# A grouped-query decode step on one core: the last head's output weights on 8 partitions, x for the end in eight loads from GpSimd

## Chip, cores and metric

One core of a Trainium2 chip, everything in float32. The metric is the device time of one execution in microseconds; the kernel before takes 1311.54 us (median of 3 runs, 1311.51 to 1311.91).

## What is computed

```python
def reference(A_x, A_k_cache, A_v_cache, A_wq, A_wo, B_x, B_w1, B_b1, B_w2, B_b2):
    # _A_ref: B=2 rows, Hq=32 heads, Hkv=8, Sk=32768 cached positions, Dh=128, D=512
    q = (x @ wq).reshape(B, Sq, Hq, Dh).transpose(0, 2, 1, 3)
    scores = einsum("bhqd,bhkd->bhqk", q, k) * (Dh ** -0.5)
    p = softmax(scores, axis=-1)
    o = einsum("bhqk,bhkd->bhqd", p, v)
    s = o.transpose(0, 2, 1, 3).reshape(B, Sq, Hq * Dh) @ wo
    # _B_ref: F=1792
    h = x @ w1 + b1
    h = max(h, 0) ** 2
    g = silu(h @ w2 + b2)
    # together; _A_ref is given layernorm(x), _B_ref too
    return x + s * g
```

The caches are 256 MiB each, wq and wo 8 MiB each, w1 and w2 3.5 MiB each; all of them are read once.

## The kernel before

There are 16 sequences `s` (8 key heads times 2 batch rows), each with 32768 cached rows. Keys come as halves of 16384 rows (`load_k`, 8 MB), cut into four tiles `n` for `scores`; values come as two chunks a sequence (`load_v`, 8 MB). All these loads, and those of the weights, are issued by SyncE in the order of the list `loads`; an entry is issued once its event is past (`give`), and `issue` goes on down the list until it meets one whose event is not. One load is split over the 16 DMA engines, 8 partitions each, and each engine works through its share of the queue in order.

Memory: `kslots` is [128, 3, 8192] floats, three slots of 4 MB for keys; `vbuf` is 8 MB for values and, at the start, for wq, w1 and w2. At the end the slots take wo: groups 0 and 1 in slot 2, groups 2 and 3 in slot 0, slot 1 is then free. The last but one value load goes into slots 0 and 1.

`scores(n)` transposes the keys 32x32 on VectorE (L248) and multiplies on TensorE (L253). `softmax` and `probs` make the weights `pT`, `values(n)` multiplies them with the values (L316) and, at the end of a sequence, forms the head outputs `oT` (L327, L328). For every second key head it spreads the 8 heads of a group for the final projection: a product with a selection mask (L332), one matmul (L335) and a copy (L336) bring row 8p+j of the group to partition p, step j of `oW`. This fits a load of wo where partition p holds the 8 consecutive rows 8p to 8p+7.

The final projection `project` (L395 to L403) runs over 4 groups of 8 steps j. A step is four matmuls, one for each quarter `g` of the 512 output columns, which go to four column groups of 32 of the array and so to four partition groups of one accumulator `a_ps`. A float32 matmul appears as two records in the trace, so a step has 8. The last group's weights come in four loads (`PIECES`), of 4, 2, 1 and 1 rows a partition, and are multiplied piece by piece. Then VectorE multiplies with the gate (L406), adds x, which lies in `xe` in the same four partition groups (L407), and two stores go out.

x for the end is loaded in four loads by ScalarE's queue at the start (L78), after b1, b2 and the x of the layer norm. GpSimd clears `oW` at the start (L180) and later, in `set_q`, places the queries of each sequence (L231). VectorE makes the selection masks (L166 to L177) among the steps of the layer norm; the reciprocal of the norm is at L197.

The order of instructions within an engine's queue is made by a scheduler that follows the program's order but moves an instruction into a wait that it foresees. Waits are semaphores; each DMA is given one of eight for SyncE and ScalarE, in turn, and one of eight others when GpSimd issues it.

Of the kernel before, what the change touches and what calls it, by code (L numbers as in the profile page):

```python
# [9 lines left out]
F32 = mybir.dt.float32  # L10
AF = mybir.ActivationFunctionType
ALU = mybir.AluOpType
AX = mybir.AxisListType

P = 128
# [10 lines left out]
NG = 4  # L26
# [3 lines left out]
TS = (1, 0, 2, 3)  # L30
NT = 4
HALF = 64 * 128
PIECES = ((0, 4), (4, 6), (6, 7), (7, 8))


@with_exitstack
def gqa_decode_kernel(ctx: ExitStack, tc: tile.TileContext, x, kc, vc, wq, wo, w1, b1, w2, b2, out):
    nc = tc.nc
    B, _, D = x.shape
    _, HKV, SK, DH = kc.shape  # L40
    HQ = wq.shape[1] // DH
# [7 lines left out]
    DE = D // NG  # L49
    WG = 8  # L50
    NWG = HQ // WG
# [3 lines left out]
    x2 = x.rearrange("b s d -> (b s) d")  # L55
    out2 = out.rearrange("b s d -> (b s) d")

    const = ctx.enter_context(tc.tile_pool(name="const", bufs=1))
    ktpool = ctx.enter_context(tc.tile_pool(name="ktpool", bufs=8))
    work = ctx.enter_context(tc.tile_pool(name="work", bufs=2))  # L60
# [3 lines left out]
    def misc(name):  # L64
        return pms.tile([P, 512], F32, tag="ms", name=name)
# [8 lines left out]
    nc.scalar.dma_start(b2t, b2[None, :])  # L74
    xe = const.tile([P, DE], F32, name="xe")
    nc.gpsimd.memset(xe, 0.0)
    for g in range(NG):
        nc.scalar.dma_start(xe[32 * g:32 * g + B, :], x2[:, g * DE:(g + 1) * DE])  # L78

    tiles = {}  # L80

# [35 lines left out]
        return t.rearrange("p (j e) -> p j e", j=FJ)  # L117


    def load_wo(i):  # L120
        if i % 2 == 0:
            wide[i // 2] = kslots[:, 2 - i].rearrange("p (i j e) -> p i j e", i=2, j=WG)
        t = wide[i // 2][:, i % 2]
        src = wo[i * WG * P:(i + 1) * WG * P, :].rearrange("(p j) e -> p j e", p=P)
        if i < NWG - 1:
            nc.sync.dma_start(t, src)
        else:
            for j0, j1 in PIECES:
                nc.sync.dma_start(t[:, j0:j1, :], src[:, j0:j1, :])  # L129
        return t  # L130

    wide = {}
    NK, NV = NS * NT, NS * NCH
    kslots = const.tile([P, 3, HALF], F32, name="kslots")
    vbuf = const.tile([P, 2 * HALF], F32, name="vbuf")
    loads = [(None, load_wq, 0), (None, load_half, 0), (None, load_half, 1), (("q", 0), load_w1, 0),
             (("s", 0), load_half, 2), (None, load_half, 3), (("q", 0), load_w2, 0)]
    for m in range(2, NV):
        loads += [(("s", 2 * m - 2), load_k, m), (("v", m - 3) if m > 2 else ("w", 1), load_v, m - 2)]
    loads += [(("s", NK - 2), load_v, NV - 2), (("v", NV - 3), load_v, NV - 1)]  # L140
    loads += [(("s", NK - 1), load_wo, 0), (("s", NK - 1), load_wo, 1), (("v", NV - 2), load_wo, 2), (("v", NV - 2), load_wo, 3)]
    past = {None}
    done = [0]
# [7 lines left out]
    def take(f, a):  # L151
        return tiles.pop((f, a))

    def give(*event):
        past.add(event)
        issue()
# [4 lines left out]
    ident = const.tile([P, P], F32, name="ident")  # L161
# [12 lines left out]
    selj = const.tile([P, WG], F32, name="selj")  # L174
    nc.vector.tensor_reduce(selj, ident.rearrange("p (e j) -> p j e", j=WG), axis=AX.X, op=ALU.add)
    sele = const.tile([P, P // WG], F32, name="sele")
    nc.vector.tensor_reduce(sele, ident.rearrange("p (e j) -> p e j", j=WG), axis=AX.X, op=ALU.add)  # L177
    oT = const.tile([P, HQ, B], F32, name="oT")
    oW = const.tile([P, NWG, WG, 32], F32, name="oW")
    nc.gpsimd.memset(oW, 0.0)  # L180
    sc = [pone.tile([P, 512], F32, tag=f"sc{i}", name=f"sc{i}") for i in range(NT)]
    o_ps = [pone.tile([P, 512], F32, tag=f"o{i}", name=f"o_ps{i}") for i in range(2)]
    for t in o_ps:
        nc.vector.memset(t, 0.0)


    st = const.tile([P, 4], F32, name="st")
# [12 lines left out]
    t_ps = misc("xnT_ps")  # L200
# [6 lines left out]
    for d in range(ND):  # L207
        for f in range(2):
            for g in range(NG):
                cc = f * NG + g  # L210
                nc.tensor.matmul(sc[f][32 * g:32 * g + 32, :], xnT[:, d, 0:32], wqt[:, d, cc * 512:(cc + 1) * 512],  # L211
                                 start=(d == 0), stop=(d == ND - 1))
    give("q", 0)
    qT = const.tile([P, B, HKV, REP, 4], F32, name="qT")
    for f in range(2):
        for h in range(REP):
# [3 lines left out]
            t_ps = misc(f"qT_ps{f}_{h}")  # L220
# [87 lines left out]
    def values(n):  # L308
        s, k = divmod(n, NCH)
        vt = take(load_v, n)  # L310
        o = o_ps[s % 2]
        for c in range(2):
            for i in range(NO // 4):
                for g in range(NG):
                    lo = (c * NG + g) * NO + 4 * i
                    nc.tensor.matmul(o[32 * g:32 * g + 16, :], pT[s][:, k, g, c, 4 * i:4 * i + 4, :].rearrange("p o h -> p (o h)"),  # L316
                                     vt[:, lo:lo + 4, :].rearrange("p o d -> p (o d)"),
                                     start=(k + c + i == 0), stop=(k == NCH - 1 and c == 1 and i == NO // 4 - 1))
        give("v", n)
        if k == NCH - 1:  # L320
            hkv, b = divmod(s, B)
            o_sb = work.tile([P, 512], F32, tag="o_sb", bufs=1, name=f"o_sb{s}")
            nc.scalar.copy(o_sb, o)  # L323
            t_ps = misc(f"oT_ps{s}")
            r4 = rs.pop(s)
            for i in range(4):
                nc.tensor.matmul(t_ps[:, :REP], o_sb[:, i * DH:(i + 1) * DH], r4[:, i, :], start=(i == 0), stop=(i == 3))  # L327
            nc.vector.tensor_copy(oT[:, hkv * REP:(hkv + 1) * REP, b], t_ps[:, :REP])  # L328
            if hkv % 2 == 1:
                i = hkv // 2  # L330
                m = work.tile([P, WG, P // WG], F32, tag="om", bufs=1, name=f"om{s}")
                nc.vector.tensor_mul(m, oT[:, i * WG:(i + 1) * WG, b:b + 1].to_broadcast([P, WG, P // WG]),  # L332
                                     sele[:, None, :].to_broadcast([P, WG, P // WG]))
                t_ps = misc(f"oW_ps{s}")
                nc.tensor.matmul(t_ps[:, :WG], m.rearrange("p h e -> p (h e)"), selj, start=True, stop=True)  # L335
                nc.scalar.copy(oW[:, i, :, b], t_ps[:, :WG])  # L336


    hT, gate = first[:, 3, :FJ * 32].rearrange("p (j b) -> p j b", j=FJ), const.tile([P, DE], F32, name="gate")
# [33 lines left out]
    for n in range(NK):  # L373
        s, i = divmod(n, NT)
        if i == 0:
            set_q(s)
        scores(n)
        if n == 1:
            mlp_up()
        if n == 3:  # L380
            mlp_down()
        if i == 3:
            softmax(s)
        if n >= 5 and n % 2 == 1:
            values((n - 5) // 2)
        if i == 3:
            probs(s)
    values(NV - 2)
    values(NV - 1)


    a_ps = sc[0]
    wot = [take(load_wo, i) for i in range(NWG)]

    def project(i, j0, j1):  # L395
        for j in range(j0, j1):
            for g in range(NG):
                nc.tensor.matmul(a_ps[32 * g:32 * g + 32, :DE], oW[:, i, j, :], wot[i][:, j, g * DE:(g + 1) * DE],
                                 start=(i == 0 and j == 0), stop=(i == NWG - 1 and j == WG - 1))

    for i in range(NWG - 1):
        project(i, 0, WG)
    for j0, j1 in PIECES:  # L403
        project(NWG - 1, j0, j1)
    asb = work.tile([P, DE], F32, tag="e", bufs=1, name="a_sb")
    nc.vector.tensor_mul(asb, gate, a_ps[:, :DE])  # L406
    nc.vector.tensor_add(xe, asb, xe)  # L407
# [25 lines left out]
```

## Time and profile before

| | |
|---|---|
| median of 3 runs | 1311.54 us |
| the profiled execution | 1311.62 us |
| its span | 1309.61 us |
| mean granted clock of TensorE | 0.841 of full speed |
| TensorE busy (matmul) | 885.4 us, 68% |
| VectorE busy | 648.8 us, 50% |
| ScalarE busy | 88.3 us, 7% |
| GpSimd busy | 15.1 us, 1% |
| read from memory | 561.01 MB, 428 GB/s over the span |
| SyncE's queue (q1) | 99.2% of the time of 16 DMA engines |

The span is what the profile covers; the execution is some 2 us longer. Busy shares are means over the whole span: an engine at 68% can still be the one that ends last in a stage, and in this profile the waits of the last 75 us are what tells. The chain of waits is the sequence of work that ended last, followed back from the end. The clock is what TensorE was granted; the last 10 us ran at 1.00.

### The profile page before, as it was taken

How to read it: one execution, taken by the hardware profiler on the slowest of the kernel's cores; microseconds unless marked ns; L12 is line 12 of the kernel's file. 1: busy time of each engine (PE TensorE's matmuls, PEld its weight loads, DVE VectorE, ACT ScalarE, POOL GpSimd, SP SyncE). 2: the span in 40 equal slices, each digit the busy share in tenths (PEclk: the TensorE clock that was granted, in tenths of full speed). 3: DMA queues.
4: the chain of work that ended last, by engine and by line, in shares of the span. 5: the costliest groups of instructions: out<-in, count | busy, mean ns of one | idle time of the engine just before them, and what ended most of it. 6: DMA issues, size and time to landing. Idle time of an engine off the chain costs nothing.

```text
span 1309.6 us, 11506 instructions
## 1 busy us (share of the span) xinstructions
PE 885.4 (68%) x4926; PEld 251.1 (19%) x4926; DVE 648.8 (50%) x742; ACT 88.3 (7%) x237; POOL 15.1 (1%) x76
## 2 busy tenths in 40 slices
PE   3867675658757567775657766566875756776575
PEld 1222121112212111121212211111221211112123
DVE  2855654435555344655435565443655534465410
ACT  0010010101001010000101001010000101000010
POOL 0000000000000000000000000000000000000000
PEclk9988877888878788877789978778987878888788
DMA  9999999999999999999999999999999999999997
GB/s 403 433 441 439 424 439 423 441 433 431 435 427 435 435 427 443 423 439 428 437 429 431 435 427 443 419 443 429 435 435 427 439 427 437 435 425 441 421 441 303
DMA packets 11040, 561.74 MB, mean 429 GB/s; under 512 B 1239, under 2 KB 1259, under 8 KB 1646
## 3 DMA queue, kind: packets, MB, share of 16 engines
q1 hardware_dynamic: 10952, 561.00, 99.2%
q8 instruction: 38, 0.62, 0.2%
q14 instruction: 12, 0.10, 0.0%
q10 hardware_dynamic: 38, 0.02, 0.0%
HBM read 561.01 MB, written 0.00 MB: 428 GB/s over the span
## 4 chain that ended last, share of the span: by engine, by line
DMA 74%; DVE 18%; issue 5%; PE 2%; SPq 0%; DVEq 0%
DMA kslots<-in_A_k_cache 68%; DVE kt L248 18%; DMA kslots<-in_A_wo 2%; DMA kslots<-in_A_v_cache 2%; DMA vbuf<-in_A_wq 2%; PE sc L211 1%; PE o_ps L316 0%; PE h_ps L347 0%; SPq L129 0%; DVE qr L218 0%; DVEq L248 0%; PE qT_ps L222 0%; PE sc L253 0%; DVE h L354 0%; DVE first L355 0%
## 5 line engine op out<-in xcount | busy, mean ns | idle before, releaser
L253 PE MATMUL sc<-kt,qz 128*32 128x512 f32 x2048 | 578.4, 671 | 330.6 <-DVE kt L248 309.0
L248 DVE STREAM_TRANSPOSE kt<-kslots 128x1024 f32<-128x1024 f32 x512 | 580.7, 1205 | 350.9 <-DMA kslots<-in_A_k_cache 350.9
L253 PEld LDWEIGHTS sc<-kt,qz 128*32 128x32 f32 x2048 | 112.0, 115 | 783.1 <-DVE kt L248 580.7
L316 PE MATMUL o_ps<-vbuf,pT 128*16 128x512 f32 x1984 | 228.8, 597 | 11.0 <-DMA vbuf<-in_A_v_cache 11.0
L316 PEld LDWEIGHTS o_ps<-vbuf,pT 128*16 128x16 f32 x1984 | 76.7, 97 | 139.9 <-issue 119.6
L275 ACT ACTIVATE p<-sc,nm 128x512 f32<-128x512 f32 x32 | 23.3, 746 | 991.0 <-DVE nm L271 991.0
L328 DVE COPY oT<-oT_ps 128x4 f32<-128x4 f32 x16 | 2.6, 162 | 121.5 <-PE oT_ps L327 121.5
L258 DVE TENSOR_REDUCE rm<-sc 128x1 f32<-128x512 f32 x32 | 22.1, 691 | 63.9 <-PE sc L253 63.9
L294 ACT COPY pT<-pT_ps 64x256 f32<-64x256 f32 x128 | 46.8, 366 | 19.7 <-PE pT_ps L290 18.2
L300 DVE RECIPROCAL r<-l_ps 128x4 f32<-128x4 f32 x16 | 2.9, 182 | 46.2 <-PE l_ps L298 46.2
L231 POOL COPY qz<-qT 32x16 f32<-32x16 f32 x64 | 12.7, 198 | 1077.4 <-PE sc L253 1042.5
L327 PE MATMUL oT_ps<-rs,o_sb 128*128 128x4 f32 x128 | 16.9, 255 | 11.5 <-ACT o_sb L323 11.4
L290 PE MATMUL pT_ps<-ident,p 128*128 128x128 f32 x128 | 20.2, 309 | 2.9 <-ACT p L275 2.9
L327 PEld LDWEIGHTS oT_ps<-rs,o_sb 128*128 128x128 f32 x128 | 15.5, 191 | 25.6 <-ACT o_sb L323 25.6
L298 PE MATMUL l_ps<-lh,ones 128*128 128x4 f32 x32 | 8.2, 327 | 17.6 <-ACT pT L294 17.6
L290 PEld LDWEIGHTS pT_ps<-ident,p 128*128 128x128 f32 x128 | 17.4, 169 | 3.1 <-ACT p L275 3.1
L323 ACT COPY o_sb<-o_ps 128x512 f32<-128x512 f32 x16 | 9.4, 585 | 100.1 <-PE o_ps L316 100.1
L278 DVE TENSOR_REDUCE l<-l 128x1 f32<-128x2 f32 x16 | 2.5, 155 | 26.9 <-ACT p L275 26.9
L264 PE MATMUL mx_ps<-ident,rm 128*128 128x128 f32 x16 | 5.2, 323 | 14.6 <-DVE rm L262 14.6
L202 PE MATMUL xnT_ps<-ident,xn 128*128 128x128 f32 x4 | 1.1, 428 | 20.4 <-DVE xn L198 20.4
L316 PE MATMUL o_ps<-kslots,pT 128*16 128x512 f32 x64 | 8.4, 682 | 4.2 <-DMA kslots<-in_A_v_cache 4.2
L298 PEld LDWEIGHTS l_ps<-lh,ones 128*128 128x128 f32 x32 | 6.8, 266 | 22.0 <-ACT pT L294 22.0
(68 smaller groups left out, 116.2 us busy)
## 6 DMA issues: line engine op xcount, KB each, us to landing
kslots<-in_A_k_cache SPq DMA_DIRECT2D x4, 4096.0 KB, 20.8
vbuf<-in_B_w SPq DMA_DIRECT2D x2, 3584.0 KB
kslots<-in_A_wo SPq DMA_DIRECT2D x3, 2048.0 KB
kslots<-in_A_wo SPq DMA_DIRECT2D x1, 1024.0 KB
kslots<-in_A_wo SPq DMA_DIRECT2D x1, 512.0 KB
kslots<-in_A_wo SPq DMA_DIRECT2D x2, 256.0 KB, 31.3
vbuf<-in_A_v_cache SPq DMA_DIRECT2D x31, 31.0
kslots<-in_A_k_cache SPq DMA_DIRECT2D x30
```

The costliest lines, as they stand in the source:

```text
L211: nc.tensor.matmul(sc[f][32 * g:32 * g + 32, :], xnT[:, d, 0:32], wqt[:, d, cc * 512:(cc + 1) * 512], start=(d == 0), stop=(d == ND - 1))
L231: nc.gpsimd.tensor_copy(qz[s % 2][32 * a:32 * a + 32, 16:].rearrange("p (e y) -> p e y", e=4)[:, :, a * REP:(a + 1) * REP], qT[32 * a:32 * ...
L248: nc.vector.transpose(r.rearrange("p e o w -> p o e w"), kt[:, g * NO:(g + 1) * NO, e0 * 32:(e0 + 2) * 32].rearrange("p o (e w) -> p o e w ...
L253: nc.tensor.matmul(bank[32 * g:32 * g + 32, :], qz[s % 2][:, lo + 32 * (e0 + e):lo + 32 * (e0 + e) + 32], kts[g][:, e].rearrange("p o w -> ...
L258: nc.vector.tensor_reduce(rm[s][:, u:u + 1], bank, axis=AX.X, op=ALU.max)
L275: nc.scalar.activation(p[:, :, :, u], sc[2 * (s % 2) + u].rearrange("p (o w) -> p o w", w=32), AF.Exp, bias=nm, scale=SCALE, accum_out=l2[ ...
L290: nc.tensor.transpose(t_ps[:, j * P:(j + 1) * P], p[:, o:o + 2].rearrange("p o w u -> p (o w u)"), ident)
L294: nc.scalar.copy(sb[64 * a:64 * a + 64].rearrange("p k g c (i j o) h -> p i o j (g c) k h", i=2, o=2)[:, i, o], v[:, :, :, :, a])
L298: nc.tensor.matmul(t_ps[:, :REP], ones, lh, start=True, stop=True)
L316: nc.tensor.matmul(o[32 * g:32 * g + 16, :], pT[s][:, k, g, c, 4 * i:4 * i + 4, :].rearrange("p o h -> p (o h)"), vt[:, lo:lo + 4, :].rear ...
L323: nc.scalar.copy(o_sb, o)
L327: nc.tensor.matmul(t_ps[:, :REP], o_sb[:, i * DH:(i + 1) * DH], r4[:, i, :], start=(i == 0), stop=(i == 3))
```

## The change

The last group's weights (heads 24 to 31) come in other pieces. Heads 24 to 27 are one load of 4 rows a partition, 28 and 29 one of 2 rows, 30 one of 1 row, each with its rows consecutive within the piece. Head 31 is a load of its own, issued ahead of these: 8 partitions of slot 1 take 16 consecutive rows each (32 KB), in the order of an access pattern of two times four. Its outputs are spread over 8 partitions and 16 steps (`oF`), and its projection is 16 steps over 8 partitions, between the first piece and the second. The spread of the last key head becomes three spreads; head 30 needs none. `oW` has 16 columns a step instead of 32, and the projection writes 16 partitions of each group. x for the end comes in eight loads of two times 64 floats, issued by GpSimd behind its other work at the start. Three pairs of masks are added.

```diff
-PIECES = ((0, 4), (4, 6), (6, 7), (7, 8))
+PIECES = ((0, 4, 0), (4, 2, 4), (6, 1, 6))
...
-    for g in range(NG):
-        nc.scalar.dma_start(xe[32 * g:32 * g + B, :], x2[:, g * DE:(g + 1) * DE])
...
-            for j0, j1 in PIECES:
-                nc.sync.dma_start(t[:, j0:j1, :], src[:, j0:j1, :])
+            base = (HQ - 1) * P
+            nc.sync.dma_start(few, wo[base:base + P, :].rearrange("(n y j) e -> y n (j e)", y=2, j=16))
+            for h0, nh, j0 in PIECES:
+                base = (i * WG + h0) * P
+                nc.sync.dma_start(t[:, j0:j0 + nh, :], wo[base:base + nh * P, :].rearrange("(p j) e -> p j e", p=P))
...
+    few = kslots[0:8, 1, :]
...
+    sels = {}
+    for nh in (16, 4, 2):
+        sels[nh] = const.tile([P, P // nh + nh], F32, name=f"sel_{nh}")
+        nc.vector.tensor_reduce(sels[nh][:, 0:P // nh], ident.rearrange("p (e j) -> p e j", j=nh), axis=AX.X, op=ALU.add)
+        nc.vector.tensor_reduce(sels[nh][:, P // nh:], ident.rearrange("p (e j) -> p j e", j=nh), axis=AX.X, op=ALU.add)
     oT = const.tile([P, HQ, B], F32, name="oT")
-    oW = const.tile([P, NWG, WG, 32], F32, name="oW")
+    oW = const.tile([P, NWG, WG, 16], F32, name="oW")
     nc.gpsimd.memset(oW, 0.0)
+    oF = const.tile([8, 16, 16], F32, name="oF")
+    nc.gpsimd.memset(oF, 0.0)
...
+    for g in range(NG):
+        for h in range(2):
+            nc.gpsimd.dma_start(xe[32 * g:32 * g + B, h * 64:h * 64 + 64], x2[:, g * DE + h * 64:g * DE + h * 64 + 64])
...
+                def spread(h0, nh, se, sj, x0):
+                    m = work.tile([P, P], F32, tag="om", bufs=1, name=f"om{s}_{h0}")
+                    nc.vector.tensor_mul(m.rearrange("p (h e) -> p h e", h=nh),
+                                         oT[:, h0:h0 + nh, b:b + 1].to_broadcast([P, nh, P // nh]),
+                                         se[:, None, :].to_broadcast([P, nh, P // nh]))
+                    nc.tensor.matmul(t_ps[:, x0:x0 + nh], m, sj, start=True, stop=True)
+
+                if i < NWG - 1:
+                    spread(i * WG, WG, sele, selj, 0)
+                    nc.scalar.copy(oW[:, i, :, b], t_ps[:, :WG])
+                else:
+                    for h0, nh, j0 in PIECES[:-1]:
+                        spread(i * WG + h0, nh, sels[nh][:, 0:P // nh], sels[nh][:, P // nh:], j0)
+                    h0, _, x0 = PIECES[-1]
+                    nc.scalar.copy(oW[:, i, 0:x0, b], t_ps[:, :x0])
+                    nc.vector.tensor_copy(oW[:, i, x0, b:b + 1], oT[:, i * WG + h0, b:b + 1])
+                    m = work.tile([P, P], F32, tag="om", bufs=1, name=f"om{s}_few")
+                    nc.vector.tensor_mul(m[:, 0:8].rearrange("p (y n) -> p y n", y=2),
+                                         oT[:, HQ - 1:HQ, b:b + 1].to_broadcast([P, 2, 4]),
+                                         sels[16][:, 0:8].rearrange("p (n y) -> p y n", y=2))
+                    nc.tensor.matmul(t_ps[0:8, 16:32], m[:, 0:8], sels[16][:, 8:], start=True, stop=True)
+                    nc.scalar.copy(oF[:, :, b], t_ps[0:8, 16:32])
...
-    def project(i, j0, j1):
+    def project(ow, wt, j0, j1, start=False, stop=False):
         for j in range(j0, j1):
             for g in range(NG):
-                nc.tensor.matmul(a_ps[32 * g:32 * g + 32, :DE], oW[:, i, j, :], wot[i][:, j, g * DE:(g + 1) * DE],
-                                 start=(i == 0 and j == 0), stop=(i == NWG - 1 and j == WG - 1))
+                nc.tensor.matmul(a_ps[32 * g:32 * g + 16, :DE], ow[:, j, :], wt[:, j, g * DE:(g + 1) * DE],
+                                 start=start and j == j0, stop=stop and j == j1 - 1)
 
     for i in range(NWG - 1):
-        project(i, 0, WG)
-    for j0, j1 in PIECES:
-        project(NWG - 1, j0, j1)
+        project(oW[:, i], wot[i], 0, WG, start=(i == 0))
+    h0, nh, j0 = PIECES[0]
+    project(oW[:, NWG - 1], wot[NWG - 1], j0, j0 + nh)
+    project(oF, few.rearrange("p (j e) -> p j e", j=16), 0, 16)
+    for h0, nh, j0 in PIECES[1:]:
+        project(oW[:, NWG - 1], wot[NWG - 1], j0, j0 + nh, stop=(j0 + nh == WG - 1))
```

## The prediction

> **What bounds the kernel now.** I read the page first: its header, the row of DMA shares in 40 slices, and the queues.
>
> ```profile
> span 1309.6 us, 11506 instructions
> DMA  9999999999999999999999999999999999999997
> q1 hardware_dynamic: 10952, 561.00, 99.2%
> ```
>
> SyncE's queue moves 561 MB and keeps the 16 DMA engines busy from the first slice to the last, so only two things can move the time: a gap in that stream, and what happens after it runs out. I therefore read the chain of waits over the last 75 us, then TensorE's timeline there.
>
> ```profile
> 1237.06 29.45 DMA kslots<-in_A_v_cache
> ...
> 1266.55 5.03 PE o_ps L316 x32
> ...
> 1274.05 31.46 DMA kslots<-in_A_wo
> 1305.50 0.04 issue
> 1305.55 0.47 PE sc L398 x8
> ```
>
> ```profile
> 1297.66 2.61 PE L398 MATMUL sc<-kslots,oW 128*32 128x128 f32 x88
> 1300.55 1.95 PE L398 MATMUL sc<-kslots,oW 128*32 128x128 f32 x64 [0.28 <-DMA kslots<-in_A_wo]
> 1303.10 2.23 PE L398 MATMUL sc<-kslots,oW 128*32 128x128 f32 x56 [0.60 <-DMA kslots<-in_A_wo]
> 1305.55 0.42 PE L398 MATMUL sc<-kslots,oW 128*32 128x128 f32 x8 [0.21 <-DMA kslots<-in_A_wo]
> ```
>
> Time is the first column, duration the second. In the last stage TensorE runs after the loads: it waits at 1300.55 (group 2 of wo), 1303.10 (the four-row piece of group 3), again within the x56 row, and at 1305.55 (the last one-row piece). One head costs 8 records (4 column groups, two passes). The chain ends with the last piece landing, 8 records and two VectorE operations.
>
> The single DMA packets of the trace (start, length, size, queue), followed end to start on each of the 16 engines, say more. The engines finish wo at very different times: seven at 1297.8 to 1298.8, three at 1303.2, six at 1304.8 to 1305.06. 38 packets of 16 KB from queue 8, about 1.05 us each, fall in turn on the same eight engines, four or five times each: that is their lag. The two engines that carry the first loads of one and two rows (b2, x) show no such packet in the 0.68 ms over which I can follow them without doubt, so I count them among the early seven.
>
> **The change part by part.**
>
> *Loads of group 3.* Before, each engine moved 8 packets of 8 KB (309 ns each), 8 of 4 KB (159) and twice 8 of 2 KB (84, one every 80 ns). One set of 2 KB packets goes: 8 x 0.080 = 0.64 us less on every engine. The last head comes as 32 KB rows; a 32 KB packet of the key halves took 1.213 us. Eight rows give eight such packets. How many engines share them no row shows for a source led by 2 and a tile of 8 partitions: between two engines (4 x 1.213 = 4.85 us each) and eight (1.21 each). The nearest row is the load of x, led by 2: two packets, on two engines. I take two: they end 4.85 - 0.64 = 4.2 us later, near 1302.5 to 1303, still before the six late ones, which now end at 1305.06 - 0.64 = 1304.4. The 8 KB packets on the late engines don't move, so the four-row piece still lands when it did.
>
> The Trainium skill ("DMA: Bandwidth & Descriptors", "Why a DMA increments its semaphore by 16 and not by 1") says a DMA runs on the largest number up to 16 that divides the slowest dimension of both sides, on the lowest-numbered engines: 2 and 8 give two. Its "Rules for kernel authors" warns that such an outer dimension confines a DMA to few engines, which speaks against the change: by the rule those two carry 4.85 us, the same term as mine, and it excludes the eight. The packets of b1, b2 and x (four, one and two rows) agree; none shows a mixed pair.
>
> *TensorE's work behind the loads.* The last head was 4 matmuls over 128 partitions; it becomes 16 steps of 4 over 8 partitions. No row shows a matmul of 8 rows and 128 columns. From below: 6.6 ns between records of different column groups, 128 x 6.6 = 0.84 us. From above: the projection's own rate, one set of four records each 0.109 us (64 records in 1.95 us with the tail of the last, clock 1.00), so 0.218 us a step and 16 x 0.218 = 3.49 us. Nearest is L361, one row, 128 columns, four column groups: its two sets start 0.113 us apart. I take 3.49.
>
> Project's order is: four-row piece, `few`, two-row piece, one-row piece. So from 1303.10 TensorE has 4 + 16 + 2 + 1 = 23 steps and every load it needs is there before its turn (`few` by 1299, the two-row piece at 1303.8, the last, 0.5 us after its bytes as now, at 1304.9): 46 sets, the last starting at 1303.10 + 45 x 0.109 = 1308.01. Before, the last set started at 1305.68. **Term: +2.35 us** (+2.33 unrounded, and a little for the switches). The cover that is gone are the waits for the pieces; the 0.64 us gained by the DMA buys nothing once TensorE ends last.
>
> *Spreading the last heads.* Sequence 15 had one spread (multiply 0.29, two matmuls 0.39, copy 0.17); it gets three through one buffer, so each multiply waits for the matmul before: about 0.9 us each, 1.8 more. Behind them in TensorE's queue stand the projections of groups 0 to 2, and TensorE waits 0.28 + 0.60 us before 1303.10 in these rows alone (about 1.2 us of no record). Before, projection records were placed between the transposing steps (18 and 22 of them), which hides most of it. Taken as 0; up to +0.7 if nothing is placed between. For sequence 14 the same work lies at 1258, with TensorE then waiting for values until 1266.55: 0.
>
> *Issue of `few`.* It stands ahead of the pieces on SyncE and writes slot 1, free only after all 64 records of values(30), 1274.9, instead of after 32:
>
> ```profile
> 1271.88 2.61 SPq L129 DMA_DIRECT2D kslots<-in_A_wo  x4
> ```
>
> Behind it wait three pieces, then issued by about 1277. Their first packets start at 1292.7 (the early engines); the last value load and 6 MB of wo stand before. Cost 0; without that backlog some 3 us.
>
> *Start.* Four issues leave ScalarE's queue (1.32 us); its next work waits until 18.69. Eight loads go on GpSimd, behind its memsets and ahead of set_q:
>
> ```profile
> 2.07 0.94 POOL L180 MEMSET oW<- 128x1024 f32 x1
> 35.02 2.00 POOL L231 COPY qz<-qT 32x16 f32<-32x16 f32 x8 [32.02 <-ACT qT L225]
> ```
>
> No row shows a DMA from GpSimd. From below: ScalarE's issues, 0.3 us each, 2.4 us. From above: each load waits for its own data behind two 64 KB packets (2.42 us each): 8 x 4.84 = 38.7 us. Against the 32 us that GpSimd idles, and being issues, they are nearest to ScalarE's: 0.
>
> The Trainium skill ("DMA: Bandwidth & Descriptors", "Anatomy of one DMA") gives about 2.0 us fixed per DMA of this path; eight in a row would be an estimated 16 us, which also ends before 35.
>
> VectorE gets six more reductions before the reciprocal, 0.28 us apart by these rows:
>
> ```profile
> 19.13 0.37 DVE L175 TENSOR_REDUCE selj<-ident 128x8 f32<-128x128 f32 x1
> 19.41 0.28 DVE L177 TENSOR_REDUCE sele<-ident 128x16 f32<-128x128 f32 x1
> 19.61 0.16 DVE L197 RECIPROCAL st<-st 128x1 f32<-128x1 f32 x1
> ```
>
> 1.7 us, of which TensorE's wait for wq (0.7 us beyond the copy at 21.57) takes a part: about 1.0 late from there. What is late next is the third key half:
>
> ```profile
> 45.67 0.80 SPq L96 DMA_DIRECT2D kslots<-in_A_k_cache  x2
> ```
>
> The first engine ran out of earlier packets at 49.48, and the first issue of all took 1.04 us to its first packet: 49.48 - 45.67 - 1.04 = 2.8 us of margin. Cost 0; beyond 2.8 us each us late is a us lost.
>
> *End.* `xe` now comes under eight semaphores. SyncE's closing waits take 62 ns each, two semaphores at a time; four more cost 0 (ahead of the output's landing) to 0.25: taken 0.12. VectorE's fit beside L406.
>
> **Sum.** +2.35 + 0.12 = +2.47. The profiled execution took 1311.62 with a span of 1309.61, 0.08 above the median; span 1312.1, median 1311.54 + 2.47 = **1314.0**. A change of 0.2% (2.62 us, 1308.92 to 1314.16) is about the least that can be told from none; the forecast lies just inside.
>
> **The rivals.**
> - *TensorE places `few` earlier.* As the 18 and 22 records above show, records are moved into waits. If `few` runs from 1302.34, before the four-row piece, 0.76 us is saved: 1313.2. Against: all write one accumulator. 0.10.
> - *The load is spread wider than two engines*, so late ones get a 32 KB packet ahead of the four-row piece: +1.21, 1315.2. The change then doesn't do what it says. 0.09.
> - *Spreads stall* TensorE past 1303.10: 1314.6. 0.07.
> - *GpSimd's loads hold up set_q*: one after the other to their landing, free at 3 + 38.7 = 41.7, 6.7 late, 3.9 beyond the margin: 1317.9. It decides once GpSimd is still issuing at 37.8. 0.07. This is the case well on the slower side.
> - *The matmuls of 8 rows run at the issue rate* (0.84 us): TensorE is done with `few` at 1303.97 + 0.84 = 1304.81, starts its last set at 1304.81 + 5 x 0.109 = 1305.36 instead of 1305.68, with every load there by 1304.9: not slower, 1311.3 with the 0.12. L361 speaks against. 0.08.
> - *The granted clock falls to half during `few`*, as it does after long idling (0.50 from 1266 to 1269): +3.4, 1317.4. The waits here are under 0.8 us. 0.04.
>
> **How the numbers follow.** The forecast has 0.55; its own spread, 1313.4 to 1314.7, puts a third of it above 1314.16. Slower: 0.18 + 0.09 + 0.07 + 0.07 + 0.04 = 0.45, of which I leave 0.01; same: 0.37 + 0.10 + 0.08 = 0.55, less 0.02 kept for a gain that I have no mechanism for (with the 0.01: faster 0.03). The range reaches from below the issue-rate case to beyond the wide load: 1310.8 to 1316.0; outside are the GpSimd and clock cases.
>
> **What would show it.** Right: 46 sets without a gap from about 1303.1, L406 near 1308.4, 32 KB packets on two engines only, set_q at about 36. Wrong: L406 before 1306.1, the four-row piece landing later, a gap in the stream near 49 us, or GpSimd busy past 37.

## The result, and the profile after

| | before | after |
|---|---|---|
| median | 1311.53 us (1311.42 to 1312.0, 6 runs) | 1316.38 us (1315.04 to 1317.69, 6 runs) |
| ratio | | 1.0035 [1.0022, 1.0048] |
| the profiled execution | 1311.62 us | 1315.04 us |
| its span | 1309.61 us | 1313.3 us |

The change makes the kernel slower by 4.85 us; 2.47 was forecast, and the time lies 0.4 us above the range. The runs after scatter over 2.7 us, those before over 0.6, and the profiled execution is the fastest of the six.

The end of the chain of waits after (start, duration, engine and line):

```profile
span 1313.3 us, 11796 instructions
...
1286.11 9.67 PE o_ps L333 x64
...
1299.38 10.14 PE sc L433 x327
1309.55 0.06 DVE a_sb L444
1309.95 0.29 DVE xe L445
```

Before, the chain went through a DMA load of wo (1274.05, 31.46 us), and TensorE had 8 records left behind it. Now no load of wo stands in the chain: from the last values (L333) on, TensorE's own work ends last. Its timeline after, where a row names tiles, shapes and the number of records:

```profile
1299.24 5.17 PE L433 MATMUL sc<-kslots,oW 128*16 128x128 f32 x176
1304.34 3.90 PE L433 MATMUL sc<-kslots,oF 8*16 8x128 f32 x128
1308.17 1.34 PE L433 MATMUL sc<-kslots,oW 128*16 128x128 f32 x24
```

None of the three rows has a wait in brackets, where every row of before from 1300.55 on had one. `few` takes 1304.34 to 1308.17, 3.83 us for 16 steps. The last six sets (a set is four records, one for each column group) are the surprise: they take 1.34 us, where the same x24 row takes 0.85 in the runs over 32 and 64 partitions below. The windows say why (start:end, length, busy time and records of PE, PEld, DVE, ACT, POOL, then the granted clock, the DMA share and GB/s):

```profile
1306.20:1308.10 1.90, 1.90 (x70) 1.74 (x62) 0.00 (x0) 0.00 (x0) 0.00 (x0) 1.00 0.03 9
1308.10:1309.50 1.40, 1.40 (x26) 0.82 (x24) 0.00 (x0) 0.00 (x0) 0.00 (x0) 0.60 0.00 0
```

TensorE is busy for all of both windows, and still the granted clock falls from 1.00 to 0.60 on the mean of the second. Record by record the sets start 0.11 us apart up to the one of 1308.40 and 0.213 apart from it on: half the clock, granted from 1308.38 on.

At the start of the run, everything is about as late as was forecast, and harmless (timeline rows of SyncE's queue, GpSimd and VectorE after):

```profile
46.75 0.80 SPq L96 DMA_DIRECT2D kslots<-in_A_k_cache  x2
```

```profile
2.81 4.22 POOL L201 DMA_DIRECT2D xe<-in_A_x  x8
36.10 1.99 POOL L248 COPY qz<-qT 32x16 f32<-32x16 f32 x8 [29.07 <-ACT qT L242]
```

```profile
20.79 0.16 DVE L214 RECIPROCAL st<-st 128x1 f32<-128x1 f32 x1
```

GpSimd's eight issues take 4.22 us, not 38.7; the reciprocal is 1.18 us later, set_q 1.08, the third key half 1.08, inside the 2.8 us of margin, and the stream has no gap there. The last head's load ran as eight 32 KB packets of 1.213 to 1.222 us, two at a time and each starting where one before it ended, so on two engines (1292.96 to 1298.3), and the last packets of wo were done at 1304.62 instead of 1305.06.

### The profile page after: what moved, and what is told of

Read it like the earlier page. It is cut to its first block, busy times and chain, and to the rows that moved or that the text cites. A ratio compares the mean times of both kernels' runs of the same rounds, so it can differ in the third digit from the quotient of the medians.

```text
span 1313.3 us, 11796 instructions
## 1 busy us (share of the span) xinstructions
PE 891.2 (68%) x5054; PEld 252.2 (19%) x5054; DVE 651.2 (50%) x754; ACT 88.6 (7%) x239; POOL 19.1 (1%) x85
## 4 chain that ended last, share of the span: by engine, by line
DMA 71%; DVE 19%; issue 5%; PE 4%; DVEq 0%; ACTq 0%; ACT 0%
DMA kslots<-in_A_k_cache 68%; DVE kt L265 18%; DMA vbuf<-in_A_v_cache 2%; PE o_ps L333 1%; DMA first<-in_A_x 1%; PE sc L433 1%; PE sc L228 1%; PE sc L270 0%; PE h_ps L382 0%; DVE qr L235 0%; PE qT_ps L239 0%; DVEq L265 0%; PE xnT_ps L219 0%; PE oT_ps L344 0%; DVE h L389 0%
## 5 line engine op out<-in xcount | busy, mean ns | idle before, releaser
L333 PE MATMUL o_ps<-vbuf,pT 128*16 128x512 f32 x1984 | 228.8, 598 | 10.3 <-DMA vbuf<-in_A_v_cache 10.3
L333 PEld LDWEIGHTS o_ps<-vbuf,pT 128*16 128x16 f32 x1984 | 74.0, 97 | 142.6 <-issue 120.3
L333 PE MATMUL o_ps<-kslots,pT 128*16 128x512 f32 x64 | 9.1, 729 | 4.8 <-DMA kslots<-in_A_v_cache 4.8
```

## The experiments

Each time stands beside runs of the kernel before on the same chip: 1311.59 us in the first group (22 runs), 1311.58 in the second (29), 1311.60 in the third (21), 1311.64 in the fourth (21). An edit is shown against the changed kernel where nothing else is said, and `...` stands for lines left out.

### First group: is it the work on TensorE, and is it the clock?

**The changed kernel again.**

> The changed kernel once more, for a second profile. Theory A (the clock): TensorE's granted clock falls to half at the end of a stretch of some 3.4 us that is filled by the matmuls of 8 rows, and it depends on the phase of that stretch how much of the last 25 us of TensorE's work runs at half; then a profile that takes 1316 us or more shows sets 0.213 us apart from a point inside few's 16 steps, earlier than 1308.4, and the times spread over 2 us or more. Theory B (the start of the last values): the spread comes from how long the last value product (64 records after 11 us of idling) runs at half clock; then the late profile has few's sets 0.109 us apart throughout, and the lateness is there by 1299.

1315.53 us (1314.85 to 1316.1, 6 runs), ratio 1.003 [1.0018, 1.0041]. Its trace has the same fall, at 1308.57, just after `few` ended. The scatter is 1.3 us, not the 2 or more of theory A. The profiled run is one of the faster (1315.08), so a late profile, which was to decide between A and B, was not had; the next two runs decide.

**The same 16 steps over 128 partitions.** The rows of `oF` below the first eight are zero.

```diff
+    few_all = kslots[:, 1, :]
...
-    oF = const.tile([8, 16, 16], F32, name="oF")
+    oF = const.tile([P, 16, 16], F32, name="oF")
...
-                    nc.scalar.copy(oF[:, :, b], t_ps[0:8, 16:32])
+                    nc.scalar.copy(oF[0:8, :, b], t_ps[0:8, 16:32])
...
-    project(oF, few.rearrange("p (j e) -> p j e", j=16), 0, 16)
+    project(oF, few_all.rearrange("p (j e) -> p j e", j=16), 0, 16)
```

> Head 31's 16 steps run over all 128 partitions: oF is zero below the first 8, and the 120 other rows of slot 1 are old values, so the result is the same with the same number of matmuls. A: no fall of the clock; 46 sets 0.109 us apart from 1303.1, 1313.9 to 1314.6, all runs within 0.9 us. B: nothing changes, median 1316.4, runs over 2.6 us. If the matmuls of 8 rows cost no clock, the two are equal.

1314.46 us (1314.3 to 1315.07, 11 runs), ratio 1.0022 [1.0013, 1.0031]. Its windows:

```profile
1306.50:1308.50 2.00, 2.00 (x81) 1.99 (x74) 0.00 (x0) 0.00 (x0) 0.00 (x0) 1.00 0.00 0
1308.50:1310.00 1.50, 0.36 (x10) 0.08 (x1) 0.58 (x2) 0.00 (x0) 0.00 (x0) 1.00 0.00 0
```

The clock stays at 1.00 to the end, and the scatter shrinks from 1.3 to 0.8 us. As many matmuls, with more rows, are 1.07 us faster, though the added rows of `oF` are zero. What is left, +2.87, is the longer work on TensorE, with whatever the rest of the change costs.

**The 16 steps twice.** Head 31 is counted twice in the output.

```diff
-    project(oF, few.rearrange("p (j e) -> p j e", j=16), 0, 16)
+    for _ in range(2):
+        project(oF, few.rearrange("p (j e) -> p j e", j=16), 0, 16)
```

> The 16 steps of head 31 are done twice (the output counts that head twice). A: the clock must fall within the 7 us at the latest, and stays at half: half of the steps or more cost double, and the 24 records behind too, so 1321.5 to 1324, 5 to 8 us over the changed kernel, with a granted clock of 0.50 in the second half. B: 32 sets at 0.109 us more, +3.5, 1319.9 and the clock at 1.00.

1322.9 us (1321.57 to 1324.04, 4 runs), ratio 1.0086 [1.0072, 1.01]. Windows:

```profile
1304.50:1306.50 2.00, 1.66 (x62) 1.37 (x54) 0.00 (x0) 0.00 (x0) 0.00 (x0) 1.00 0.00 0
1306.50:1308.50 2.00, 2.00 (x48) 1.75 (x44) 0.00 (x0) 0.00 (x0) 0.00 (x0) 0.52 0.03 8
1308.50:1311.00 2.50, 2.50 (x56) 2.16 (x52) 0.00 (x0) 0.00 (x0) 0.00 (x0) 0.50 0.03 7
1311.00:1314.00 3.00, 3.00 (x64) 2.60 (x60) 0.00 (x0) 0.00 (x0) 0.00 (x0) 0.50 0.00 0
```

Once fallen, at 1306.58, the clock stays at half for as long as 8-row matmuls run, though TensorE is busy without a pause. Idling is not the cause. The second 16 steps cost 7.4 us over the first, more than twice the 3.49 of full clock, since part of the first falls under the half clock too.

**Without the 64 matmuls of the last head.** Head 31 is left out of the sum; its load and its spread stay.

```diff
-    project(oF, few.rearrange("p (j e) -> p j e", j=16), 0, 16)
```

> The 64 matmuls of head 31 are left out (the output lacks that head), the loads and spreads stay. A and B both: TensorE has 7 steps after 1303.1 instead of 23, waits for the pieces again, and ends by the loads: 1311.0 to 1311.6, runs within 0.6 us. If the lost time lies in the loads, in the spreads or at the start instead, it stays above 1313.

1311.08 us (1310.89 to 1311.38, 11 runs), ratio 0.9997 [0.9988, 1.0006]. TensorE waits for the loads again:

```profile
1303.23 1.07 PE L433 MATMUL sc<-kslots,oW 128*16 128x128 f32 x32 [0.52 <-DMA kslots<-in_A_wo]
1304.49 1.04 PE L433 MATMUL sc<-kslots,oW 128*16 128x128 f32 x24 [0.19 <-DMA kslots<-in_A_wo]
```

The four-row piece lands at about 1303.2 (before: 1303.1), and 4.45 us of the changed kernel hang on these 64 matmuls. The 0.5 us below before is what the lighter stream gave here, less what the rest of the change costs.

### Second group: rows, the rest of the change, and other layouts

**32 and 64 partitions.** As the run over 128, with 32 and with 64.

> As the changed kernel, but the 16 steps run over 32 partitions (24 of them zero in oF). A1: the clock falls by the number of rows in use: with 32 of 128 it falls as with 8, so 1315.0 to 1317.7 with a spread of over 1 us, and a profile with 0.50 behind few. A2: one full row of the array's blocks counts as in use: no fall, 1314.3 to 1315.1, as with 128 rows.

> The same over 64 partitions. A1: between: if the fall needs less than about half of the rows, no fall and 1314.3 to 1315.1; if it falls too, 1315.0 to 1317.7. A2: no fall, 1314.3 to 1315.1.

Over 32: 1315.59 us (1314.4 to 1316.39, 7 runs), 1.0029 [1.0018, 1.0039], like 8 rows in time and scatter. Over 64: 1314.6 us (1314.29 to 1314.79, 11 runs), 1.0023 [1.0014, 1.0032], like 128. By the times, the change of behaviour lies between 32 and 64 rows. One window over 64, then the same over 32:

```profile
1306.50:1308.40 1.90, 1.90 (x70) 1.67 (x62) 0.00 (x0) 0.00 (x0) 0.00 (x0) 1.00 0.00 0
```

```profile
1306.50:1308.40 1.90, 1.90 (x76) 1.69 (x68) 0.00 (x0) 0.00 (x0) 0.00 (x0) 1.00 0.00 0
```

The profiled execution over 32 (1314.76) shows no fall of the clock, which A1 had expected, so for 32 the statement rests on the times.

**x alone.** The kernel before, with x in the eight loads from GpSimd.

```diff
-    for g in range(NG):
-        nc.scalar.dma_start(xe[32 * g:32 * g + B, :], x2[:, g * DE:(g + 1) * DE])
...
+    for g in range(NG):
+        for h in range(2):
+            nc.gpsimd.dma_start(xe[32 * g:32 * g + B, h * 64:h * 64 + 64], x2[:, g * DE + h * 64:g * DE + h * 64 + 64])
```

> The kernel before with one part of the change alone: x for the end in eight loads from GpSimd. Theory A (the whole loss lies in TensorE's work at the end: 3.27 us more matmuls, the fall of the clock, a wait for instructions): no change, 1311.3 to 1311.9, within 0.2 us of before. Rival C (the start or the closing waits cost part of it): 0.3 us or more over before.

1311.81 us (1311.54 to 1312.18, 11 runs), ratio 1.0002 [0.9993, 1.001]: +0.23, which the interval does not tell from nothing and which lies between theory A's 0.2 and rival C's 0.3. The trace shows most of it: VectorE's two last operations start 0.40 apart instead of 0.32, with four waits on semaphores before the second instead of one, and from the second to the end of the span it is 3.34 us instead of 3.25, where SyncE closes with eight waits instead of five:

```profile
1306.12 0.29 DVE L409 TENSOR_TENSOR a_sb<-gate,sc 128x128 f32<-128x128 f32 x1 [8.62 <-PE sc L401]
1306.52 0.29 DVE L410 TENSOR_TENSOR xe<-a_sb,xe 128x128 f32<-128x128 f32 x1
```

**The relief of the late engines without the 16 steps.** The last head as 128 rows of 2 KB, still on two engines (order 2 times 64), one step of four matmuls, spread by a permuted identity.

```diff
-            nc.sync.dma_start(few, wo[base:base + P, :].rearrange("(n y j) e -> y n (j e)", y=2, j=16))
+            nc.sync.dma_start(few, wo[base:base + P, :].rearrange("(n y) e -> y n e", y=2))
...
-    few = kslots[0:8, 1, :]
+    few = kslots[:, 1, 0:D]
...
```

> The last head on two DMA engines as in the change, but as 128 rows of 2 KB on 128 partitions: rows 0, 2, 4 and so on go to partitions 0 to 63, the odd ones to 64 to 127, and a matmul with a permuted identity brings the head's outputs into this order. One step instead of 16. A: TensorE has 8 steps after 1303.1 as before, follows the loads, and these end 0.64 us earlier: 1310.9 to 1311.3, 0.3 to 0.6 us under before, runs within 0.6 us. If loads of this form on two engines disturb the stream or these two end last, it is above 1311.6.

1313.05 us (1312.83 to 1313.25, 11 runs), ratio 1.0011 [1.0002, 1.002]: A's 1310.9 to 1311.3 failed by 2 us, and the other branch, a disturbed stream, came. TensorE waits longer for a load (group 2; before: 0.28 us):

```profile
1302.70 1.94 PE L431 MATMUL sc<-kslots,oW 128*16 128x128 f32 x64 [1.64 <-DMA kslots<-in_A_wo]
```

Packets of every size are 1.4 times as long between 1293 and 1300: at the median 16 KB takes 0.852 us instead of 0.614, 8 KB 0.445 instead of 0.309, 2 KB 0.122 instead of 0.085.

### Third and fourth group: why the other layouts slow the stream

**32 partitions of four rows** (8 KB packets, two engines), 4 steps ahead of the four-row piece, x by ScalarE as before.

```diff
...
+    few = kslots[0:32, 1, 0:4 * D]
...
+    project(oF, few.rearrange("p (j e) -> p j e", j=4), 0, 4)
     h0, nh, j0 = PIECES[0]
     project(oW[:, NWG - 1], wot[NWG - 1], j0, j0 + nh)
...
```

> A middle way: the last head on two DMA engines as 32 partitions of 4 rows (8 KB packets, 16 on each of the two), 4 steps instead of 16, multiplied ahead of the four-row piece, in the wait that TensorE has there; x for the end back in four loads on ScalarE's queue. If theory A is all: 3 steps more (0.65 us) lie in a wait of 0.77 us, no fall of the clock, the loads end 0.64 us earlier, no extra closing waits: 1310.8 to 1311.2, some 0.5 us under before. If loads on few engines that write many partitions slow the whole stream, as the packets of the 128-row form showed (all sizes 1.4 times as long from 1293 to 1300), it is over 1312 and 8 KB packets take over 400 ns again.

1314.4 us (1312.89 to 1316.31, 11 runs), ratio 1.002 [1.0011, 1.0029]: 1310.8 to 1311.2 failed too, and the branch over 1312, with 8 KB packets over 400 ns, came.

```profile
1302.98 2.88 PE L432 MATMUL sc<-kslots,oW 128*16 128x128 f32 x64 [2.00 <-DMA kslots<-in_A_wo]
```

```profile
1305.00:1308.00 3.00, 3.00 (x57) 1.80 (x52) 0.00 (x0) 0.00 (x0) 0.00 (x0) 0.50 0.22 83
```

Between 1296 and 1299, 16 KB packets take 1.09 us and 8 KB 0.571; TensorE waits 2.00 us for group 2, and from 1303.80 on works at half clock, so this time holds a clock loss as well.

**128 rows in two loads of 64 partitions**, spread over 16 engines, every other row to each half.

```diff
-            nc.sync.dma_start(few, wo[base:base + P, :].rearrange("(n y) e -> y n e", y=2))
+            for y in range(2):
+                nc.sync.dma_start(few[64 * y:64 * y + 64, :], wo[base:base + P, :].rearrange("(n y) e -> y n e", y=2)[y])
...
```

> The 128-row form again, its rows in the same order and at the same distance of 4 KB, but as two loads of 64 partitions each that go over all 16 engines. D1 (reading every other 2 KB row slows the stream): packets 1.4 times as long again, 1312.5 to 1313.3. D2 (it takes two engines that write all over the partitions): packets at 309 ns for 8 KB, 1311.3 to 1311.9, the loads ending as before but for one more load.

1313.6 us (1313.15 to 1313.92, 11 runs), ratio 1.0015 [1.0006, 1.0024], above both ranges and nearer to D1's. The packets are long again (16 KB 0.728 us in 1293 to 1296), so it does not need two engines.

**The same two loads with 64 consecutive rows each** (the edit against the run before).

```diff
-                nc.sync.dma_start(few[64 * y:64 * y + 64, :], wo[base:base + P, :].rearrange("(n y) e -> y n e", y=2)[y])
+                nc.sync.dma_start(few[64 * y:64 * y + 64, :], wo[base + 64 * y:base + 64 * y + 64, :])
...
-                    nc.tensor.matmul(t_ps[:, 16:17], perm, oT[:, HQ - 1, b:b + 1], start=True, stop=True)
+                    nc.tensor.matmul(t_ps[:, 16:17], ident, oT[:, HQ - 1, b:b + 1], start=True, stop=True)
```

> As the run in which head 31 came in two loads of 64 partitions with every other row of wo, but each load now takes 64 consecutive rows (partition 64y + n holds row 64y + n); everything is still computed. That run took 1313.6 us, with 16 KB packets of 0.728 us in 1293 to 1296 and 1299 to 1302, where 0.611 is the rule. Theory S (reading every other row of 2 KB slows the stream): the slow packets go, 16 KB packets near 0.611 from 1293 on, 1311.6 to 1312.2. Theory W (the engines write to other partitions than the eight that they write in all other loads): as slow as that run, 1313.2 to 1314.0, packets near 0.73. The DMA gain of the change, at most 0.5 us, would not show in either.

1313.44 us (1313.17 to 1313.72, 11 runs), ratio 1.0014 [1.0005, 1.0023].

```profile
1301.76 1.94 PE L430 MATMUL sc<-kslots,oW 128*16 128x128 f32 x64 [0.77 <-DMA kslots<-in_A_wo]
1305.13 1.07 PE L430 MATMUL sc<-kslots,oW 128*16 128x128 f32 x32 [1.43 <-DMA kslots<-in_A_wo]
```

The packets are as long (16 KB 0.776 us in 1293 to 1296): reading every other row is not the cause. Theory W, that engines now write to other partitions than in all other loads, is left of the two. One thing more differs: SyncE issues the last piece at 1286.01 here, at 1285.85 in the run before and at 1291.56 in the run over 128 rows on two engines, against 1277.63 in the changed kernel. The run over 32 partitions issues it at 1276.93 and has the long packets too, so a late issue is not what the four share.

**One load of 128 rows**, all else of the change kept (the edit against the run before).

```diff
-            for y in range(2):
-                nc.sync.dma_start(few[64 * y:64 * y + 64, :], wo[base + 64 * y:base + 64 * y + 64, :])
+            nc.sync.dma_start(few, wo[base:base + P, :])
```

> Everything of the change but the layout of head 31: its 128 rows come in one load of one row a partition, 16 engines, ahead of the four-row piece, and it is one step over 128 partitions; x comes in the eight loads by GpSimd, the three spreads, the masks and the 16 columns a step of oW are those of the changed kernel; everything is computed. Theory (the rest of the change costs only its longer end, +0.23 us as in the run with x alone): 1311.6 to 1312.0. Rival (the spreads or the new order of the pieces cost something by themselves, which would be part of the changed kernel's time too): 1312.3 or more, with TensorE later than 1303.3 at the four-row piece.

1311.99 us (1311.74 to 1312.34, 11 runs), ratio 1.0003 [0.9994, 1.0012]. The packets have their usual length again (16 KB 0.613), so a load of 128 partitions does no harm where two of 64 do.

```profile
1303.91 0.79 PEld L429 LDWEIGHTS sc<-kslots,oW 128*16 128x16 f32 x32 [0.35 <-DMA kslots<-in_A_wo]
```

```profile
1299.52 5.46 PE L429 MATMUL sc<-kslots,oW 128*16 128x128 f32 x180
1304.80 0.40 PE L429 MATMUL sc<-kslots,oF 128*16 128x128 f32 x8
1305.17 1.25 PE L429 MATMUL sc<-kslots,oW 128*16 128x128 f32 x24
```

Everything of the change but the 8-partition layout costs 0.35 us, which the interval does not tell from nothing, and the run with x alone had 0.23. That leaves some 0.12 for the spreads and the new order. TensorE reaches the four-row piece at 1303.91, later than the 1303.3 that the rival named, but what holds it there is the load: the weights wait 0.35 us for wo, since head 31's rows are issued ahead of the piece. No matmul row has a wait from 1299.52 on, and that is the clock as much as the spreads: it rose to 1.00 at 1291.43 in this trace and at 1289.69 before, and the last values end 1.0 us later.

## Why the prediction failed, step by step

**Right.** What bounds the kernel, and that the bound moves from the loads to TensorE: the chain shows it, and so does the run without the 64 matmuls. The two engines for `few`; the relief of the late ones (0.44 us, forecast 0.64), which buys nothing; the four-row piece at 1303.2; the issue of `few` behind values(30); the start, to a tenth of a us in set_q. Of the rivals, none of these happened: `few` placed earlier, a wider load, GpSimd holding set_q, the issue rate.

**Right in its price, with some luck.** The spreads were taken as 0, up to 0.7. From the end of the last values to TensorE's first unbroken row of the projection it is 3.46 us after (1295.78 to 1299.24) and 2.86 before (1294.80 to 1297.66), so they take 0.6 us of TensorE. That is hidden where the clock rises early: in the run with the steps twice (rise at 1289.52) TensorE still waits 0.48 us for the four-row piece. In the trace after it rises at 1291.32, the values end 1 us later than before, and TensorE comes to the piece without a wait, at 1303.24.

**Mis-sized, by little.** In the trace after, the last set starts at 1309.04, not 1308.01. Of the 1.03 us, 0.14 is the later start at 1303.24, 0.57 is lost around `few` (1303.24 + 40 x 0.109 = 1307.60, against 1308.17), most of it at the two changes between the tiles, where 0.20 us lie between the last record of one and the first of the next (I had put this at "a little"), and 0.32 is the clock (five sets in 0.87 us instead of 0.55). Behind the last set come 0.15 more by the clock, 0.08 at VectorE and 0.06 at the close; the last two are 0.14 where 0.12 was taken. So 2.33 + 1.03 + 0.15 + 0.14 = 3.65, the growth of the span (1309.61 to 1313.26). This is the fastest of the six runs; the median is 1.34 us above it.

**The step that failed** is the rate of `few` and of the pieces behind it, "one set of four records each 0.109 us", for which I took the clock 1.00 as given to the end. The rival for it, "The granted clock falls to half during `few`", I set aside with "The waits here are under 0.8 us" and 0.04: I knew only idling as a cause. There are no waits at all, and the clock falls all the same, because the matmuls use 8 rows. The run over 128 rows, same matmuls and order, shows what the forecast would have been worth without it: +2.87, or 1314.46, within the forecast's own 1313.4 to 1314.7. The fall adds 0.9 to 1.1 us in the repeat (3.94, less 3.02 of 64 rows and 2.87 of 128) and 1.8 to 2.0 in the first six runs (4.85, less the same), not the 3.4 of the rival.

**Why it scatters.** Three traces have the fall at 1306.58, 1308.38 and 1308.57, which is 2.6 to 4.2 us after `few` began, and in the last two just after it ended. The clock's rise after the cold stretch before, at 1289.52, 1291.32 and 1291.50, lies 17.07 us earlier each time, which is five times 3.413; and in each of the fourteen traces all changes of the clock lie on one grid of 3.413 us, to 3 ns. So these are fixed windows, whose place against the program differs from run to run. If a window of few rows ends late in `few`, little is left to run at half clock; if early, more. The rise shows in the windows of the trace after, too:

```profile
1286.00:1289.00 3.00, 2.89 (x16) 0.66 (x20) 0.00 (x0) 0.00 (x0) 0.00 (x0) 0.50 1.02 437
1289.00:1292.00 3.00, 3.00 (x20) 0.61 (x16) 0.00 (x0) 0.00 (x0) 0.00 (x0) 0.61 1.01 431
```

The Trainium skill ("TensorE: Matmul & The Clock Gate", Part 1) gives such a window, 3413 ns and free-running, and these traces agree with it. It says that the clock goes by how busy TensorE has been, and warns of idle gaps over some 3.4 us; by that rule the clock would have stayed up, and here the measurement decides: 0.50 for seven us of the run with the steps twice, in which TensorE was busy throughout.

**Open.** No trace was taken of the slowest runs (up to 1317.69); that a still earlier fall makes them is argued from the windows, not shown. No number of rows between 32 and 64 was tried, and the run over 32 was traced once, without a fall.

## What to carry to other kernels

Count a matmul's rows, not only its columns: matmuls over few partitions cost as much time as full ones, and several us of them in a row can halve TensorE's clock for what follows; zero rows up to 64 partitions avoided that here at no cost. Relieving a queue pays only up to the wait that ends last behind it (here 0.5 us), so price the work that the relief puts on the next engine at its measured rate first. A load that covers fewer partitions, or goes over fewer engines, can slow the transfers beside it: look at the packets' length, not only at their number.

## What the runs showed of the hardware beside this

**Rows and clock.** 8 rows: clock 0.50 under full load. 64 and 128 rows: 1.00. 32 rows: the times and the scatter of 8. How busy TensorE is does not sort the 3.413 us windows from 1298 on into those after which the clock fell and those after which it stayed: with 3.41 us busy (8 rows) and 3.07 (the steps twice) it fell, with 1.51 (over 128 rows, the last window) and 1.78 (128 rows on two engines) it stayed. Rows nearly do: count the matmul records that start in a window, each by its share of 128 rows, and the clock fell at 0 to 36 and once at 44, and stayed at 42 to 110. The traced window over 32 rows comes to 46, because 0.7 us of it are full matmuls; 32-row sets alone would come to about 31 (3.413 / 0.109 x 4 x 32 / 128), 64-row sets to 63. This is an estimate from one stage of these traces, which no run was made to test.

**Partitions of a load.** Two loads over 64 partitions on 16 engines, read with gaps or without, one over 128 on two engines and one over 32 on two engines lengthen the 16 KB packets 1.2 to 1.8 times for some us, and others with them, and cost 1.5 to 2.8 us against before (1313.05 to 1314.4, the last with a clock loss); one over 128 on 16 engines (1311.99) and the change's own over 8 (16 KB 0.611 to 0.614 us beside it) do not. The Trainium skill ("DMA: Bandwidth & Descriptors", "The descriptor swizzle") says that in a load of 128 partitions each engine writes to a port of its own: engine 0 to partitions 0 to 3 and 32 to 35, engine 1 to 4 to 7 and 36 to 39, and so on. If an engine takes its partitions in order in the other forms as well, which neither that section nor a trace says, eight partitions on two engines stay on the engines' own ports and the four slow forms do not; that fits every one of these runs. The trace doesn't show ports or which partition a packet goes to, so the cause of the long packets stays open.

**A wait for instructions.** Queue 8 carries 16 KB packets of kind "instruction": 38 before, 39 after, 40 with the steps twice. Each time 128 matmul records and as many weight loads came on top, so a packet seems to hold 256 of TensorE's instructions. In four of the six traces with `few` (the changed kernel twice, over 128 rows, twice the steps) the same record, the 31st of `few`, starts late, 0.10, 0.20, 0.45 and 0.61 us after the one before it where 0.09 is usual, and 1.3 to 1.5 us after such a packet has ended (1303.76 to 1304.13). Over 32 and 64 rows the packet ended earlier, at 1303.59, and there is no such gap. The row of the run over 128 partitions shows it as a wait on nothing visible:

```profile
1305.20 2.90 PE L434 MATMUL sc<-kslots,oF 128*16 128x128 f32 x97 [0.17 <-issue]
```

So a TensorE that no longer waits for its data can, as these times suggest, still wait for its instructions; the trace names no releaser, so this is not shown.
